# Wider shift, cheaper skip term, one more eight-residue slice and later turned rows in a fused layer-norm, long-convolution and MLP gradient kernel

## The chip, the cores and the metric

The kernel runs on one core of a Trainium2 chip. The metric is device microseconds of a whole execution, as a median over runs. Executions of the kernel before lie between about 1953 and 1974 us here, so a difference of a few microseconds needs many runs or a stage of the trace. All comparisons below are between executions in the fast state, and the one profile that fell in the slow state is marked.

TensorE is PE (its weight load PEld), VectorE is DVE, ScalarE is ACT, GpSimd is POOL, SyncE is SP. Numbers after an L are line numbers; the changed kernel's are two or three lower than those of the kernel before.

## The reference, cut to what matters

```python
# S = 2048 rows, D = 1024 channels, F = 3584; all bf16
def forward(A_q, A_k, A_v, shift_k, ssm_k, ssm_D, w_gate, w_up, w_down):
    xn = layernorm(A_q)
    k_shift = sum(pad(A_k)[t:t + S] * shift_k[:, 3 - t] for t in range(4))   # 4 taps
    kv = k_shift * A_v
    y = irfft(rfft(pad(kv, 2 * S)) * rfft(pad(ssm_k, 2 * S)))[:S]           # long convolution
    y = y + kv * ssm_D                                                     # the skip term
    s = xn * y
    h = (xn @ w_gate) * (xn @ w_up)
    return A_q + s * silu(h @ w_down)
# returned: the output and the gradients of all nine inputs for a given grad_out
```

## The kernel before

The first 550 us hold the gate and up matmuls (`psg<-wslab,U`, 192 tiles of eight matmuls after the start) and, threaded between them, the forward convolution. The channels are worked in eight slices of 128. For each pair of slices VectorE shifts k and multiplies it by v (`kv`). TensorE transforms `kv` and the filter `hx` (`psF`), ScalarE copies the result out of PSUM (`SP`), VectorE finishes the transforms and multiplies the spectra, and TensorE transforms back (`psY`). A slice is transformed with four residues or with eight: eight takes half the TensorE matmuls and more VectorE work. `hN` is the product of gate and up, made on VectorE and transposed by TensorE. The first matmul that reads all of the gated products, `psbm`, ends the stage.

```python
EIGHT = (7,)                                     # slices transformed with eight residues

def load_kv(dp, c):                              # one block of rows of a pair of slices
    k = kst.tile([P, 2, 11, P], BF16, name="k", bufs=2)
    for e in range(2):
        cld_k(k[:, e], c, 2 * dp + e)            # 128 channels, 256 B, at a time
    ...
def shift(dp):
    kv = cx.tile([P, 2, NB, P], BF16, name="kv")
    ...
    for c in range(2):                           # two blocks of rows, 2048 elements an operation
        ...
        tt(acc, k[:, :, 0:8, :], wb(3), MUL)
        for j in (2, 1, 0):
            tt(prod, k[:, :, 3 - j:11 - j, :], wb(j), MUL)
            tt(acc, acc, prod, ADD)
            yield 2.5                            # the amount of work told to the pacing
        tt(kv[:, :, 8 * c:8 * c + 8, :], acc, v..., MUL)
        st(KSHd[...], acc)                       # shifted k, for the backward pass
# cmm(), the transform of one half on TensorE: the skip term is one more matmul,
# a row of constants (one partition) by the row of ssm_D
    if first is not None and k == 0:
        nc.tensor.matmul(ps[:, 0, 0:P], wsc_row[:], first, start=False, stop=True)
# pacing: after every gate/up tile, pump() emits convolution work up to this share of its total
def tick():
    cnt[0] += 1
    pump((20.0 + (F_TOTAL - 20.0) * (cnt[0] + 4) / NT) / F_TOTAL)
# gate/up unit: product on VectorE in its fixed program order; turned five tiles later
def multiply():
    tt(hN[:, 0:n], gut[:, 0, 0:n], gut[:, 1, 0:n], MUL)
    ...
    defer(turn)
# last stage, tap gradients: turned rows loaded one block ahead
    if i < 15:
        kT, dkT = load_turned(i + 1)
```

`tt` keeps VectorE's operations in the order in which the program writes them. So the pacing decides which `hN` product stands behind which convolution operation.

## Time and profile before

| | kernel before |
|---|---|
| time | 1956.21 us median of 3 runs (1956.19 to 1961.06) |
| the profiled execution | 1968.15 us, span 1966.4, fast state |
| TensorE, VectorE, ScalarE, GpSimd busy | 98%, 77%, 33%, 18% |
| `psbm` begins | 549.4 us |
| gradient matmuls `psx<-…,dgut` | 1551.3 to 1947.9 us, with 8.2 us of waits for `dgut` |

The profiled execution is 12 us slower than the median of the timed ones, so a page's span must not be compared with another kernel's median. TensorE's busy time is modelled from its matmul records, and some records are missing: this page counts 10907 of them and 1924.2 us. A second trace of the very same kernel (run `before_again`) counts 11043 and 1931.9 us. So a change of 5 us in that line says nothing by itself. The starts of single tiles and the named waits are firmer.

### The profile page before, as it was taken

What the parts mean: (1) busy time and instruction counts of PE and PEld (TensorE: products, weight loads), DVE (VectorE), ACT (ScalarE), POOL (GpSimd) and SP (SyncE); (2) the same over time, 40 slices, a digit from 0 to 9 for tenths busy, and PEclk for the clock granted to TensorE, in tenths of its full rate; (3) what the DMA queues carried; (4) which work ended last, traced back from release to release, by engine and by line L of the source; (5) the groups of instructions that cost most, each with busy time, mean ns of one, the idle gap of its engine ahead of it and who ended that gap; (6) DMA issues with size and microseconds to landing.
All of it is one profiled execution on the core that took longest, in us unless ns stands there. A gap on an engine that the chain in (4) does not pass through costs nothing.

```text
span 1966.4 us, 27343 instructions
## 1 busy us (share of the span) xinstructions
PE 1924.2 (98%) x10907; PEld 1038.5 (53%) x11043; DVE 1523.9 (77%) x1711; ACT 639.8 (33%) x940; POOL 356.1 (18%) x529
## 2 busy tenths in 40 slices
PE   8999999999999999999999999999999999999989
PEld 4555555555444446666566666664444444444434
DVE  8699999999736555888799899999995404777763
ACT  5664555555432224333222222222212002001122
POOL 3413222121112221000122121021112001111111
PEclk8999999999999999999999999999999999999999
DMA  8967767556799988566778698575796999897993
GB/s 294 303 213 257 240 205 273 194 180 235 266 285 295 287 274 306 187 214 211 253 245 272 236 240 277 189 270 181 222 260 164 149 207 196 162 213 154 190 210 118
DMA packets 454463, 448.62 MB, mean 228 GB/s; under 512 B 282736, under 2 KB 370872, under 8 KB 440384
## 3 DMA queue, kind: packets, MB, share of 16 engines
q1 hardware_dynamic: 393088, 232.86, 47.1%
q0 software_dynamic: 44928, 184.65, 28.2%
q10 hardware_dynamic: 16320, 29.36, 4.1%
q8 instruction: 86, 1.41, 0.3%
q14 instruction: 41, 0.34, 0.1%
HBM read 198.20 MB, written 189.84 MB: 197 GB/s over the span
## 4 chain that ended last, share of the span: by engine, by line
PE 62%; issue 17%; DVE 7%; DMA 5%; POOL 4%; SPq 3%; ACT 2%; another core or an unknown queue 0%; POOLq 0%; ACTq 0%; DVEq 0%
PE psb L1256 19%; PE psb L1332 9%; PE psb L1239 9%; PE psg L617 9%; PE psx L1383 7%; PE psbm L1108 3%; SPq L1327 3%; DVE dkp L1087 2%; PE psF L231 2%; DMA HTd<-hT 1%; DVE dka L209 1%; PE psY L443 1%; DMA xn_t<-XNd 1%; DMA dkT<-DKSHd 1%; DVE W L209 1%
## 5 line engine op out<-in xcount | busy, mean ns | idle before, releaser
L617 PE MATMUL psg<-wslab,U 128*128 128x512 bf16 x1732 | 406.5, 382 | 14.4 <-ACT gut L619 6.2
L1256 PE MATMUL psb<-U,U 128*128 128x512 bf16 x1792 | 397.4, 379 | 0.0
L1383 PE MATMUL psx<-U,dgut 128*128 128x512 bf16 x1507 | 333.1, 380 | 10.5 <-DMA dgut<-DGd 8.2
L1383 PEld LDWEIGHTS <-dgut 128*128 128x128 bf16 x1792 | 175.5, 98 | 222.2 <-DMA dgut<-DGd 9.8
L617 PEld LDWEIGHTS <-U 128*128 128x128 bf16 x1792 | 173.8, 98 | 200.8 <-issue 15.3
L1256 PEld LDWEIGHTS <-U 128*128 128x128 bf16 x1792 | 175.2, 98 | 197.6
L1239 PE MATMUL psb<-wdt,U 128*128 128x256 bf16 x1792 | 205.3, 273 | 1.1 <-ACT bm L1126 1.1
L1239 PEld LDWEIGHTS <-U 128*128 128x128 bf16 x1792 | 175.3, 98 | 32.0 <-issue 1.4
L619 ACT CAST gut<-psg 128x512 bf16<-128x512 f32 x216 | 126.3, 586 | 183.7 <-PE psg L617 172.2
L1332 PE MATMUL psb<-U,U 128*128 128x512 bf16 x813 | 179.6, 379 | 1.0
L1108 PE MATMUL psbm<-U,ht 128*128 128x512 bf16 x768 | 168.9, 379 | 0.8
L1261 ACT CAST wb<-psb 128x512 bf16<-128x512 f32 x112 | 65.6, 586 | 311.1 <-PE psb L1256 295.6
L209 DVE TENSOR_TENSOR W<-W 128x1024 f32<-128x1024 f32 (+1 forms) x150 | 151.3, 1026 | 3.2
L1332 PEld LDWEIGHTS <-U 128*128 128x128 bf16 x896 | 87.4, 98 | 105.4 <-issue 1.0
L1108 PEld LDWEIGHTS <-ht 128*128 128x128 bf16 x784 | 76.6, 98 | 91.8
L1415 ACT ACTIVATE dx_t<-dxn 128x1024 bf16<-128x1024 f32 x15 | 15.9, 1057 | 331.4 <-DVE dxn L209 331.4
L1241 ACT CAST dht<-psb 128x512 bf16<-128x512 f32 x112 | 65.7, 586 | 121.3 <-PE psb L1239 120.2
L209 DVE TENSOR_TENSOR U<-U,dht 128x2048 bf16<-128x2048 bf16 x56 | 68.3, 1221 | 46.2 <-ACT dht L1241 46.1
L1087 DVE SCALAR_TENSOR_TENSOR dkp<-dkT,kT 128x1024 bf16<-128x1024 bf16 (+2 forms) x64 | 78.3, 1224 | 29.1 <-DMA dkT<-DKSHd 27.4
L209 DVE TENSOR_TENSOR dxn<-psx,dxna_t 128x1024 f32<-128x1024 f32 x15 | 18.3, 1222 | 94.7 <-PE psx L1383 80.0
L1362 ACT CAST wbs<-psb 128x512 bf16<-128x512 f32 x52 | 30.5, 586 | 148.2 <-PE psb L1332 139.2
L209 DVE TENSOR_TENSOR W<-SP 128x1024 f32<-128x1024 f32 x64 | 74.2, 1220 | 4.0 <-ACT SP L253 3.1
(243 smaller groups left out, 2383.0 us busy)
## 6 DMA issues: line engine op xcount, KB each, us to landing
U<-GUd SPq DMA_DIRECT2D x28, 1024.0 KB, 8.2
DGd<-U SPq DMA_DIRECT2D x28, 1024.0 KB, 4.8
GUd<-gut ACTq DMA_DIRECT2D x54, 512.0 KB, 5.9
out_dram<-wb SPq DMA_DIRECT2D x112, 128.0 KB, 4.3
U<-Hd SPq DMA_DIRECT2D x14, 1024.0 KB, 5.5
Hd<-hN POOLq DMA_DIRECT2D x54, 256.0 KB, 4.2
HTd<-hT POOLq DMA_DIRECT2D x54, 256.0 KB, 3.3
ht<-HTd SPq DMA_DIRECT2D x7, 1536.0 KB, 9.7
```

The lines of the kernel that those rows point to most:

```text
L209: pinned(V.tensor_tensor(o, a, b, op))
L617: gu_mm[0] = nc.tensor.matmul(ps[:], XNT[q][:, dc, qi * P:(qi + 1) * P], w[:, dc].rearrange("p a f -> p (a f)"), start=(dc == 0), stop=(dc ...
L619: nc.scalar.copy(out=gut[:, :, i], in_=ps[:].rearrange("p (a f) -> p a f", a=2))
L1087: ins = V.scalar_tensor_tensor(prod[:].rearrange("p r d -> p (r d)")[:, lo:H], dkT[:, 0, lo:H], 1.0, kT[:, 0, 13 + m + lo:13 + m + H], op0 ...
L1108: nc.tensor.matmul(ps[:, dh * 512:(dh + 1) * 512], ht(fc)[:, i * P:(i + 1) * P], WD[fc // 4][:, fc % 4, dh * 512:(dh + 1) * 512], start=(f ...
L1239: nc.tensor.matmul(ps[:, x * SLW:(x + 1) * SLW], DBMT[2 * hf + g][:, dc, (b % 4) * P:(b % 4 + 1) * P], wdt[:, dc, :], start=(dc == 0), sto ...
L1241: nc.scalar.copy(out=dht[:, 2 * e:2 * e + 2].rearrange("p b f -> p (b f)"), in_=ps[:])
L1256: nc.tensor.matmul(ps[:], XN[b // 4][:, b % 4, dc * P:(dc + 1) * P], dgus[b // 8][:, :, b % 8], start=(b == 0), stop=(b == NB - 1))
L1261: nc.scalar.copy(out=wb[:, dc % 2].rearrange("p a f -> p (a f)"), in_=ps[:])
L1327: nc.sync.dma_start_transpose(out=t[:, 2 * i:2 * i + 2], in_=DGd[2 * j + i, a, 512 * g:512 * g + 512, :])
L1332: nc.tensor.matmul(ps, h[:, b, f * P:(f + 1) * P], DBM[b // 4][:, b % 4, dh * 512:(dh + 1) * 512], start=(b == 0), stop=(b == NB - 1))
L1383: nc.tensor.matmul(ps[:, dh * 512:(dh + 1) * 512], t[n][:, f, i * P:(i + 1) * P], WGU[n][:, f, dh * 512:(dh + 1) * 512], start=(n == 0 and ...
```

## The change

The change makes the shift work on both slices of a pair and both row blocks at once (256 channels side by side, 4096 elements an operation). The skip term uses the transform's own weights by a row padded to 128 partitions (`Dz`), so no one-row weights are loaded. Slice 0 is also done with eight residues, to take matmuls from TensorE. The turned rows of the tap gradients are loaded later. The pacing constants move with it.

```diff
-    KSHd = dram.tile([8, P, NB, P], BF16, name="KSHd")
-    KSLd = dram.tile([8, S + 8, P], BF16, name="KSLd")
+    KSHd = dram.tile([4, P, NB, 256], BF16, name="KSHd")
+    KSLd = dram.tile([4, S + 8, 256], BF16, name="KSLd")
...
-                nc.tensor.matmul(ps[:, 0, 0:P], wsc_row[:], first, start=False, stop=True)
+                nc.tensor.matmul(ps[:, 0, 0:P], T[:, 0, 0, :], first, start=False, stop=True)
...
-    EIGHT = (7,)
+    EIGHT = (0, 7)
+    SHIFT_W = 8 * 2.3
...
-            for c in range(2):
-                ...                     # eight operations of 2048 elements a block
+            k = S_.pop(("k", dp))
+            wb = lambda j: Wbc[:, j:j + 1, dp * 256:(dp + 1) * 256].unsqueeze(1).to_broadcast([P, 2, 8, 256])
+            acc, prod, v = [U[i][:].rearrange("p (c r d) -> p c r d", c=2, r=8) for i in (6, 7, 4)]
+            with tc.issue_after(last.ins):
+                tt(acc, k[:, :, 0:8, :], wb(3), MUL)
+            yield 2.3
+            for j in (2, 1, 0):
+                tt(prod, k[:, :, 3 - j:11 - j, :], wb(j), MUL)
+                yield 2.3
+                tt(acc, acc, prod, ADD)
+                yield 2.3
+            tt(kv[:].rearrange("p (c r) d -> p c r d", c=2), acc, v, MUL)
+            st(KSHd[dp], U[6][:].rearrange("p (b d) -> p b d", b=NB))
...
+        Dz = cs.tile([P, D], BF16, name="Dz")
+        V.memset(Dz[:], 0.0)
+        cld(Dz[0:1, :], A_ssm_D.rearrange("(o d) -> o d", o=1))
+        nc.scalar.activation(Dz[0:1, :], Dz[0:1, :], ACT.Copy, scale=WSC)
...
-        pump((20.0 + (F_TOTAL - 20.0) * (cnt[0] + 4) / NT) / F_TOTAL)
+        pump((SHIFT_W + (F_TOTAL - SHIFT_W) * (cnt[0] + 8) / (NT + 4)) / F_TOTAL)
...
-        kT, dkT = load_turned(0)
...
+                if j == 2:
+                    kT, dkT = load_turned(i)
...
-            if i < 15:
-                kT, dkT = load_turned(i + 1)
```

More of the change, by code (lines that the diff above doesn't have):

```diff
@@ L74, in build_kernel, with cld_k @@
     cld = st
-    def cld_k(t, c, ds):
-        src = KSLd[ds]
-        cld(t, bass.AP(src.tensor, src.offset + 1024 * c * P, [[8 * P, P], [P, 11], [1, P]]))
+    def cld_k(t, c, dp):
+        src = KSLd[dp]
+        cld(t, bass.AP(src.tensor, src.offset + 1024 * c * 256, [[8 * 256, P], [256, 11], [1, 256]]))
     def cld_v(t, c, d0, w):
@@ L126, in build_kernel @@
     RSTN = const.tile([P, NB], F32, name="RSTN")
-    wsc_row = const.tile([1, P], BF16, name="wsc_row")
-    nc.vector.memset(wsc_row[:], WSC)
     Wbc = const.tile([P, 4, D], BF16, name="Wbc")
@@ L139, in zero_rows @@
         V.memset(zr[:], 0.0)
-        st(KSLd[:, 0:3, :], zr[:, 0:3, :])
+        st(KSLd[:, 0:3, :], zr[0:4].rearrange("p a x -> p (a x)")[:, 0:768].rearrange("p (a x) -> p a x", a=3))
         st(DKSHd[:, S:S + 8, :], zr[:])
@@ L649, in load_kv @@
         def load_kv(dp, c):
-            k = kst.tile([P, 2, 11, P], BF16, name="k", bufs=2)
-            for e in range(2):
-                cld_k(k[:, e], c, 2 * dp + e)
+            if c == 0:
+                S_["k", dp] = kst.tile([P, 2, 11, 256], BF16, name="k")
+            cld_k(S_["k", dp][:, c], c, dp)
             v = U[4][:, 2048 * c:2048 * c + 2048].rearrange("p (a x) -> p a x", a=8)
             cld_v(v, c, dp * 256, 256)
-            S_["kv", dp, c] = (k, v)
         def load_h(ds):
@@ L659, in load_h @@
             cld(U[5][:, 0:2048], A_ssm_k[ds * P:(ds + 1) * P, :])
-            drow = cs.tile([1, P], BF16, name="drow", bufs=2)
-            cld(drow[:], A_ssm_D[ds * P:(ds + 1) * P].rearrange("(o d) -> o d", o=1))
             S_["h", ds] = hrow
-            S_["D", ds] = drow
         def shift(dp):
-            kv = cx.tile([P, 2, NB, P], BF16, name="kv")
+            kv = cx.tile([P, NB, 256], BF16, name="kv")
             S_["kvt", dp] = kv
-            wb = lambda j: Wbc[:, j, dp * 256:(dp + 1) * 256].rearrange("p (e d) -> p e d", e=2).unsqueeze(2).to_broadcast([P, 2, 8, P])
-            for c in range(2):
-                k, v = S_.pop(("kv", dp, c))
-                acc = U[7 - c][:, 0:2048].rearrange("p (e r d) -> p e r d", e=2, r=8)
-                with tc.issue_after(last.ins):
-                    tt(acc, k[:, :, 0:8, :], wb(3), MUL)
-                for j in (2, 1, 0):
-                    prod = U[7][:, 2048:4096].rearrange("p (e r d) -> p e r d", e=2, r=8)
-                    tt(prod, k[:, :, 3 - j:11 - j, :], wb(j), MUL)
-                    tt(acc, acc, prod, ADD)
-                    yield 2.5
-                tt(kv[:, :, 8 * c:8 * c + 8, :], acc, v.rearrange("p r (e d) -> p e r d", e=2), MUL)
-                st(KSHd[2 * dp:2 * dp + 2, :, 8 * c:8 * c + 8, :].rearrange("e u b d -> u e b d"), acc)
-                yield 2.5
+            k = S_.pop(("k", dp))
[11 more added lines that the diff above has]
+            st(KSHd[dp], U[6][:].rearrange("p (b d) -> p b d", b=NB))
+            yield 2.3
         def h_rows(ds):
@@ L699, in kvs @@
         def kvs(ds):
-            return S_["kvt", ds // 2][:, ds % 2]
+            return S_["kvt", ds // 2][:, :, ds % 2 * P:(ds % 2 + 1) * P]
         def tail(ds):
@@ L763, in conv_forward @@
                     load_kv(ds // 2 + 1, c)
-            D0 = S_.pop(("D", ds))[:]
+            D0 = Dz[:, ds * P:(ds + 1) * P]
             sph = []
@@ L796, in conv_forward @@
         kst.release()
-    F_TOTAL = 4 * 20.0 + 6.0 + 8 * (0.5 + FWD4_W + 1.3 + PROD_W + INV_W) + 10.0 - 0.95 * 8 * (4 * 1.75 + 0.95 + 4 * 0.9)
+    F_TOTAL = 4 * SHIFT_W + 6.0 + 8 * (0.5 + FWD4_W + 1.3 + PROD_W + INV_W) + 10.0 - 0.95 * 8 * (4 * 1.75 + 0.95 + 4 * 0.9)
     F_TOTAL += len(EIGHT) * 2 * (FWD8_W - 9.6 + 0.95 * 1.75) - 2.0
@@ L812, in copy_k @@
     def copy_k(dp):
-        for ds in (2 * dp, 2 * dp + 1):
-            ld(KSLd[ds, 3:3 + S, :].rearrange("(p a) d -> p a d", a=16),
-               kin[:, ds * P:(ds + 1) * P].rearrange("(p a) d -> p a d", a=16))
+        ld(KSLd[dp, 3:3 + S, :].rearrange("(p a) d -> p a d", a=16),
+           kin[:, dp * 256:(dp + 1) * 256].rearrange("(p a) d -> p a d", a=16))
     copy_k(0)
@@ L854, in tick @@
         cnt[0] += 1
-        pump((20.0 + (F_TOTAL - 20.0) * (cnt[0] + 4) / NT) / F_TOTAL)
-    pump(20.0 / F_TOTAL)
+        pump((SHIFT_W + (F_TOTAL - SHIFT_W) * (cnt[0] + 8) / (NT + 4)) / F_TOTAL)
+    pump(SHIFT_W / F_TOTAL)
     for sl in range(2, NSL - 2):
@@ L972, in load_side @@
                 cld_v(v[:, 8 * c:8 * c + 8, :], c, ds * P, P)
-            cld(ksh[:], KSHd[ds])
+            cld(ksh[:], KSHd[ds // 2][:, :, ds % 2 * P:(ds % 2 + 1) * P])
             side_in[n] = (v, ksh)
```

## The prediction

> **What bounds the kernel now.** I read the page first (busy shares, then the chain that ended last), then busy time by stretch, then the two engines' instruction timelines where their stretches are full.
>
> The page's first line of part 1:
> ```profile
> PE 1924.2 (98%) x10907; PEld 1038.5 (53%) x11043; DVE 1523.9 (77%) x1711; ACT 639.8 (33%) x940; POOL 356.1 (18%) x529
> ```
> TensorE idles only 42 us of 1966.4 in the whole span. So the kernel is TensorE-bound on average. An average over stages hides a second limit, so next the busy times by stretch (columns: length, then busy us and instruction count of PE, PEld, DVE, ACT, POOL; clock; DMA share; GB/s):
> ```profile
> 92.00:200.00 108.00, 103.86 (x665) 59.81 (x676) 102.52 (x92) 60.48 (x82) 26.46 (x42) 1.00 0.75 244
> 200.00:300.00 100.00, 99.36 (x618) 56.77 (x629) 98.78 (x88) 55.82 (x78) 22.73 (x35) 1.00 0.67 228
> 300.00:400.00 100.00, 99.14 (x630) 57.64 (x641) 95.67 (x85) 57.16 (x80) 22.73 (x35) 1.00 0.62 219
> 400.00:545.00 145.00, 140.87 (x838) 77.19 (x852) 126.46 (x124) 75.90 (x111) 26.91 (x41) 1.00 0.68 232
> 545.00:765.00 220.00, 216.71 (x1096) 107.04 (x1114) 116.67 (x181) 61.91 (x66) 45.53 (x71) 1.00 0.95 298
> ```
> From 92 to 400 us, the stage in which the gate/up matmuls run beside the forward convolution, TensorE and VectorE are both full: 98.78 of 100 us of VectorE between 200 and 300. After 545 VectorE is half idle. Three of the four parts of the change act in that doubly full stage. The timelines show how the two are tied there (start, length, engine, line, operation; the wait in brackets):
> ```profile
> 193.02 0.61 PE L637 MATMUL tr<-ident,hN 128*128 128x128 bf16 x8
> 195.04 1.91 PE L231 MATMUL psF<-kv,TF 128*128 128x256 bf16 x16 [1.42 <-DVE kv L209]
> ...
> 193.76 1.23 DVE L209 TENSOR_TENSOR kv<-U,U 128x2048 bf16<-128x2048 bf16 x1
> ...
> 302.26 1.22 DVE L209 TENSOR_TENSOR kv<-U,U 128x2048 bf16<-128x2048 bf16 x1
> 303.93 1.91 PE L231 MATMUL psF<-kv,TF 128*128 128x256 bf16 x16
> ```
> TensorE starts on `kv` (the shifted k times v) at 195.04, when VectorE has just finished it at 194.99; the next pair is finished at 303.48 and used at 303.93. Both queues keep a fixed order, so there is next to no slack: what lengthens VectorE's work ahead of `kv` moves TensorE.
>
> **What the Trainium skill says.** "VectorE: DVE Perf Modes", Side-by-side: where the cycles go for N=2048 bf16, gives 1224 ns for a two-source bf16 operation of 2048 elements, with about 150 cycles of it fixed; the trace agrees (1218 to 1225 ns for 2048, 2284 ns for 4096). So joining two operations saves one fixed part, not half. "TensorEngine Tiling (Array Packing)", Key Properties, says that changing the tiling mode drains TensorE. The trace fits: each load of the one-row skip weights sits idle 0.21 us first. "DMA: Bandwidth & Descriptors", Specifications, puts line rate at 512 B and above; the page counts 282736 of 454463 packets under 512 B, but no wait of TensorE in this stage names the k copies.
>
> **The change, part by part.**
>
> 1. Shift. 16 operations of 2048 elements a pair of slices become 8 of 4096. One half before took 184.60 to 194.91 with one `hN` product of 0.60 in it: 9.7 us, so 19.4 us a pair; eight at 2284 ns are 18.3 us. It saves about 1.1 us of VectorE a pair, 4.4 in all, 3.3 of it after the first pair (which lies before 85 us, where VectorE waits for TensorE anyway).
>
> 2. Skip term on the transform's own weights.
> ```profile
> L236 PE MATMUL psF<-drow,wsc_row x15: 224/224/226, 99.6 to 473.1; 1*128 1x128 bf16 x15
> its engine sat idle before it (us, times) until:
>   issue: 3.1, 15
> ```
> Around one of them: two transform matmuls start at 138.72, the skip term at 139.04, the next at 139.19. Two transform matmuls cost 0.22 (16 take 1.75 from start to start), so 0.47 minus 0.22 leaves 0.25 us a term; a full-height 128-column one costs about 0.06 (8 transposes take 0.44). That saves about 0.2 us on 14 terms (one of 15 goes): 3.0 us of TensorE. The row is now loaded into a zeroed 128-row tile and scaled on ScalarE. In the built program that scaling stands in ScalarE's fixed order between two gate/up evictions and waits for the load, which waits for the clearing on VectorE. I put the clearing at about 78 us and the landing 4.1 us (the old row's median) after the issue; TensorE may wait 1 us there.
>
> 3. First slice with eight residues. TensorE loses 32 transform matmuls of 256 columns (16 on `kv`, 16 on `hx`) at 0.109 us: 3.5 us. VectorE gains: in the old kernel the last slice is already done so, and its first transform runs from 470.44 to 486.78 with one `hN` product inside, 15.7 us; the four-residue transform of slice 0 runs from 98.07 to 107.34, 9.3 us. Two transforms: +12.9 us.
>
> 4. Later turned rows. In the built program the sync queue holds the turned loads at the same places between the same `dgut` loads, and each still waits for the last tap product of the unit before. The added store waits are for stores half a millisecond old. VectorE's order after the forward stage is unchanged. I give it 0. The one large wait of the last stage therefore stays:
> ```profile
> 1882.84 0.61 PE L1383 MATMUL psx<-U,dgut 128*128 128x512 bf16 x1 [5.68 <-DMA dgut<-DGd]
> ```
> The k copies and loads get 512 B rows (off the path), while the backward reads of the stored shift get 256 B rows, 2048 a load, hidden behind prefetch.
>
> Sum for the forward stage: TensorE -6.5 us; VectorE +12.9 - 3.3 = +9.6 us after its restart at 98.07. Which of them counts is the whole question. The program's order answers: before the third slice's `kv` the changed TensorE queue has about 6.6 us more work than the old (102 against 95, from 0.216, 0.109 and 0.056 us a matmul), because the pacing puts more gate/up work there; VectorE has 12.9 - 1.1 + 0.6 (one more `hN`) = 12.4 more. TensorE, which waited 1.42 there, is now 5.8 us more ahead and waits about 7. For the pairs after it TensorE has some 6 and 4.5 us less work, VectorE only 1.1 less, so it falls short by some 4 us and 3 us again. VectorE's lag of 9 to 10 us is what remains at 415 us. It takes back part: before, it stood 2.33, 1.18 and 1.80 us waiting for gate/up evictions (315.60, 357.54, 469.83), and such waits shrink when it is the late one: -3 to -4. The stage should end 6 us later, give or take 4, with the skip row's wait in it. After 549 us TensorE is full to 1866 us, and there the delay is kept: 1956.2 + 6 = 1962. I shade it to 1961 because the pacing constants look tuned for this order.
>
> **Rivals.**
> A. TensorE alone bounds, VectorE's lag being absorbed. For it: 98% busy, and VectorE stands 5.97 and 10.15 us at the stage's end. That would give 1956.2 - 6.5 = 1950. Against: those waits lie behind the last transforms, and the `kv` hand-overs come earlier.
> B. The later turned rows free the transposing queue and the 8.2 us that TensorE waits for `dgut` between 1866 and 1898 go, alone or on top of A: 1948 or 1942. Against: queue order and waits are the same.
> C. VectorE's lag is paid in full (no waits taken back) and the skip row holds an eviction longer than thought: 1956.2 + 10 + 2 = 1968.
> D. 256 B reads in the backward stage delay its loads: VectorE has 537 of 597 us there, but TensorE waits for nothing of it; under 2 us.
>
> **Range and chances.** Most weight lies on +3 to +10, a quarter on A or a mixture, little on B and C: 1951 to 1969. A move of 2% is 39 us, six times any term, and the old runs spread by 5 us: faster 0.005, same 0.985, slower 0.01.
>
> **What would show it.** Right: in the changed profile TensorE's busy time falls by about 6 us and its waits from 92 to 550 us grow by more than 10, named after VectorE (`kv`, `hN`, `HX`) or ScalarE evictions behind it; the third slice's `kv` comes near 208; VectorE is at 98% or more of 100 to 400; the skip term's idle (3.1 us) is gone; the psbm matmuls begin near 555 instead of 549.4; from there to the end the two traces have equal length within 3 us. Wrong: psbm begins before 549, so VectorE had slack that I don't see; or the `dgut` wait near 1882 vanishes, so part 4 was not inert.

## The result, and the profile after

The changed kernel took 1966.23 us (median of 4 runs, 1963.6 to 1969.7). The kernel before took 1956.2 us in the same rounds (4 runs, 1955.88 to 1961.06). The ratio of the fast runs is 1.0047, with a 95% interval of 1.0024 to 1.0069: within 2%, but slower. (A ratio here is the mean time of one kernel's fast runs over that of the other's of the same rounds, so it is not quite the ratio of the medians.) The profiled execution took 1965.88 us, in the fast state.

The page's first line, with busy time, share and instructions of each engine:

```profile
PE 1919.2 (98%) x10875; PEld 1037.1 (53%) x11010; DVE 1532.7 (78%) x1703; ACT 639.6 (33%) x941; POOL 350.1 (18%) x510
```

VectorE has 8.8 us more than before (1523.9). Then the busy times by stretch (length; busy us and count of PE, PEld, DVE, ACT, POOL; clock; DMA share; GB/s):

```profile
92.00:200.00 108.00, 102.39 (x630) 57.03 (x640) 102.39 (x102) 58.14 (x81) 19.97 (x31) 0.98 0.65 216
200.00:300.00 100.00, 97.05 (x611) 56.65 (x620) 99.14 (x83) 55.50 (x77) 23.50 (x36) 0.98 0.73 244
300.00:400.00 100.00, 96.65 (x615) 56.63 (x626) 96.98 (x80) 56.03 (x78) 22.25 (x34) 1.00 0.65 225
```

VectorE is now the fuller of the two from 200 to 400 us, and TensorE has gaps. Two things are to be seen: TensorE's busy time falls below VectorE's, and the granted clock is 0.98 in two stretches where it was 1.00. The hand-over of the second pair, VectorE first and TensorE second (start, length, engine, line, operation, the wait in brackets):

```profile
206.34 2.29 DVE L207 TENSOR_TENSOR kv<-U,U 128x4096 bf16<-128x4096 bf16 x1
...
208.68 2.43 PE L229 MATMUL psF<-kv,TF 128*128 128x256 bf16 x16 [2.17 <-DVE kv L207]
...
315.54 1.91 PE L229 MATMUL psF<-kv,TF 128*128 128x256 bf16 x16 [1.92 <-DVE kv L207]
```

`kv` comes at 208.6, where it came at 195.0. TensorE waits 2.17 us for it, and 1.92 us for the next one, which before cost nothing. The waits of TensorE by cause, before (92 to 550 us) and after (92 to 556 us), with total, times and longest; smaller ones are left out:

```profile
PE psg L617 <- ACT gut L619: 2.8, 2, 2.2
PE psF L231 <- ACT SP L253: 1.8, 1, 1.8
PE psF L231 <- DVE kv L209: 1.4, 1, 1.4
PE tr L637 <- ACT hT L638: 1.1, 1, 1.1
PE tr L637 <- DVE hN L209: 0.4, 1, 0.4
...
```

```profile
PE tr L635 <- DVE hN L207: 5.6, 2, 3.3
PE psF L229 <- DVE kv L207: 4.8, 3, 2.2
...
PE psg L615 <- ACT gut L617: 0.6, 1, 0.6
...
```

The waits named after VectorE grew from 1.8 to 10.4 us; those for ScalarE's `gut` fell from 2.8 to 0.6. The largest is one that no hand-over of `kv` shows. VectorE had eight-residue work of slice 0 queued ahead of an `hN` product that TensorE needed:

```profile
114.79 4.63 DVE L207 TENSOR_TENSOR W<-SP 128x1024 f32<-128x1024 f32 x4
119.34 0.69 DVE L207 TENSOR_TENSOR hN<-gut 128x1024 bf16<-128x1024 bf16 x1
...
120.08 0.62 PE L635 MATMUL tr<-ident,hN 128*128 128x128 bf16 x8 [3.29 <-DVE hN L207]
120.74 3.18 PE L615 MATMUL psg<-wslab,U 128*128 128x512 bf16 x8
```

The eight matmuls after the wait take 3.18 us, where eight take 1.89 elsewhere. The stretches of 3 us after it say why; the third number from the end is the granted clock:

```profile
120.00:123.00 3.00, 2.88 (x15) 1.42 (x16) 2.97 (x5) 1.99 (x3) 1.17 (x2) 0.70 0.23 87
123.00:126.00 3.00, 3.00 (x18) 1.73 (x17) 2.96 (x6) 0.58 (x1) 0.10 (x1) 0.74 0.25 87
126.00:129.00 3.00, 2.95 (x15) 1.37 (x14) 3.00 (x6) 1.17 (x2) 0.56 (x1) 1.00 0.24 89
```

After standing still for 3.29 us TensorE runs at 0.70 and 0.74 for two stretches. That is (1 − 0.70) × 3 + (1 − 0.74) × 3 = 1.7 us more, on top of the wait. The Trainium skill has this effect: "TensorE: Matmul & The Clock Gate", What's actually happening, says that the array's clock is halved after an idle window of about 3.4 us and restored after a busy one. The size fits this trace: by an estimate from the page's figure, half speed for 3.4 us costs 1.7 us. What starts it does not quite fit; see the last section.

The ends of the stages, from the list of one tile's instructions (median duration, first and last start):

```profile
L1105 PE MATMUL psbm<-U,U x110: 379/379/379, 555.6 to 579.6; 128*128 128x512 bf16 x110
...
L1380 PE MATMUL psx<-U,dgut x1507: 376/379/380, 1558.8 to 1945.4; 128*128 128x512 bf16 x189
```

`psbm` begins at 555.6 instead of 549.4. The gradient matmuls take 386.6 us instead of 396.6, because in this execution they do not wait for `dgut`. That is why the two profiled spans (1966.4 and 1964.1) go the other way than the timed medians.

### An account of the forward stage

For every trace I split the time from the first gate/up matmul to `psbm` in three. Waits are what the profile's list of TensorE's waits sums to in that stretch. Clock is (1 − granted clock) times length, summed over stretches of 20 us. The rest is what TensorE's work takes at full clock. The rest scatters by up to 3 us among traces with the same TensorE work (515.2 to 518.1 in the first four rows).

| run | length | waits | clock | rest |
|---|---|---|---|---|
| kernel before | 539.1 | 17.5 | 6.4 | 515.2 |
| before_again (the same kernel) | 537.8 | 16.3 | 3.4 | 518.1 |
| only_turned | 540.1 | 16.7 | 8.2 | 515.2 |
| only_shift | 536.2 | 18.4 | 0.0 | 517.8 |
| only_skip | 540.2 | 22.8 | 3.4 | 514.0 |
| eight7 | 544.4 | 22.5 | 8.8 | 513.1 |
| eight7_pace | 538.6 | 20.2 | 5.0 | 513.4 |
| changed kernel | 545.3 | 27.2 | 8.8 | 509.3 |
| after_pace | 540.9 | 24.3 | 5.0 | 511.6 |
| less_dve | 538.7 | 21.9 | 5.4 | 511.4 |
| less_dve2 | 535.9 | 18.5 | 5.4 | 512.0 |
| three8 | 555.4 | 35.9 | 12.2 | 507.3 |
| pool_gate | 574.7 | 46.8 | 17.6 | 510.3 |

From before to changed: rest −5.9, waits +9.7, clock +2.4, together +6.2 us. Of the waits' 9.7, 1.6 are waits for the first weights (`wslab`), which vary from 0 to 3.2 us among the traces.

After `psbm`, the fast traces with under 2 us of waits for `dgut` need 1407 to 1411 us to the end of the span, the changed kernel's 1408.5 included. The kernel before needed 1417.0 in its profiled execution and 1422.1 in before_again, less_dve2 1417.6.

### The profile page after: what moved, and what is told of

It is laid out like the page before. It is cut to its first block, busy times and chain, and to the rows that moved or that the text cites. A ratio compares the mean times of both kernels' runs of the same rounds, so it can differ in the third digit from the quotient of the medians.

```text
span 1964.1 us, 27240 instructions
## 1 busy us (share of the span) xinstructions
PE 1919.2 (98%) x10875; PEld 1037.1 (53%) x11010; DVE 1532.7 (78%) x1703; ACT 639.6 (33%) x941; POOL 350.1 (18%) x510
## 4 chain that ended last, share of the span: by engine, by line
PE 72%; issue 12%; DVE 8%; DMA 3%; POOL 3%; ACT 1%; another core or an unknown queue 0%; SPq 0%; POOLq 0%; ACTq 0%; DVEq 0%
PE psx L1380 20%; PE psb L1253 19%; PE psb L1329 9%; PE psb L1236 9%; PE psbm L1105 6%; PE psg L615 5%; DVE W L207 2%; DVE U L207 1%; DVE HX L207 1%; PE psF L229 1%; DVE KX L207 1%; PE psY L1034 1%; DMA XNd<-U 1%; PE psY L430 1%; DMA U<-in_A_v_dram 1%
## 5 line engine op out<-in xcount | busy, mean ns | idle before, releaser
L207 DVE TENSOR_TENSOR W<-W 128x1024 f32<-128x1024 f32 (+1 forms) x156 | 156.5, 1020 | 3.4
## 6 DMA issues: line engine op xcount, KB each, us to landing
GUd<-gut ACTq DMA_DIRECT2D x54, 512.0 KB, 5.5
```

The lines of the kernel that those rows point to most:

```text
L207: pinned(V.tensor_tensor(o, a, b, op))
```

## The experiments

Twelve kernels ran in three groups, each group on one chip with its own runs of the kernel before (medians 1959.41, 1958.74 and 1958.13 us; 46, 67 and 43 runs). The theory is that VectorE's extra work for slice 0 lengthens the forward stage. The rivals are the new layout, the skip row, the pacing, the turned rows, and TensorE alone.

"First `kv` to `psbm`" runs from the end of VectorE's first whole `kv` to the start of `psbm`: 464.7 us in the kernel before (465.2 in before_again), 473.7 in the changed kernel. The changed kernel's first `kv` ends 2.8 us sooner after the first gate/up matmul (71.6 against 74.4 us), so this measure shows a loss of 9.0 us where the whole stage shows 6.2.

### before_again: what two executions of one kernel differ by

No edit.

> The old kernel once more, for the spread and for the wait for dgut. Its first profile held 8.2 us of waits for dgut after 1866 us and a time of 1968.15, while its timed runs were at 1956. Theory: the wait belongs to that one execution; this profile has less than 2 us of it and a span near 1955. Rival: the wait is a fixed part of the kernel, and returns with 6 to 9 us. The ratio to the old kernel should be 1.000 within 0.002.

Measured: 1958.9 us (14 runs), ratio 1.0001 (0.9986 to 1.0017). Its profiled execution took 1970.45 us and waited for `dgut` again, six times:

```profile
PE psx L1383 <- DMA dgut<-DGd: 6.9, 6, 2.7
```

My expectation of under 2 us was wrong. Eight other fast traces, some with the old loads (only_shift, only_skip) and some with the new, have no such wait. So it comes and goes from execution to execution, and one pair of profiles can't show that a change removed it. Still, waits of more than 2 us in total were seen only with the old loads, in 2 of 4 fast traces, and in none of 9 with the new; that the later loads make the wait rarer isn't excluded.

### only_eight: part 3 alone

```diff
-    EIGHT = (7,)
+    EIGHT = (0, 7)
```

> The old kernel with eight residues in the first slice as the only change. Theory: VectorE +12.9, TensorE -3.5, and no shift to take 3.3 back: psbm starts 8 to 11 us later than the old 549.4, the time is 1964 to 1968, as bad as the whole change or worse. Rival (TensorE bounds): 3.5 us faster, 1952 to 1953.

Measured: 1964.4 us (17 runs), ratio 1.0025 (1.0015 to 1.0034). The theory's 1964 is just met, but over this group's base of 1959.41: the loss is 4.9 us by the ratio, half of the whole change's 9.2, and not "as bad or worse". The rival's 1952 is out: with 3.5 us less for TensorE to do the kernel is slower. (`EIGHT` also enters `F_TOTAL`, the total of the pacing, so the pacing shifts a little with it.) Its profiled run fell in the slow state (1990.55 us), so I take nothing from its trace.

### only_shift: part 1 alone

The change's `KSHd`, `KSLd`, `load_kv` and `shift` with `EIGHT = (7,)`, the old pacing offset, skip row and turned rows.

> The kernel before with part 1 of the change alone (two slices side by side, 256 channels a row; old residues, old pacing offset, old skip row, old turned rows). Theory (the extra eight-residue slice on VectorE is the whole loss, and the new layout is harmless or a little good): VectorE busy 2 to 5 us less than before (1523.9), TensorE busy unchanged within 1.5 us of 1924, first kv to the gate matmuls (psbm) 463 to 465 us against 464.7 and 465.2 for the kernel before, time within 3 us of it. Rival (the layout itself costs: one wait for both row blocks, U6/U7/U4 freed later, 256-byte reads in the last stage): first kv to psbm 468 or more, or psbm to the end of the last gradient matmuls 4 us or more longer than before.

Measured: 1958.62 us (22 runs), ratio 1.0010 (0.9991 to 1.0029). VectorE is busy 1519.6 us, 4.3 less. First `kv` to `psbm` took 464.5 us. The layout is harmless and no gain: the saved VectorE time is not where the path is, since here TensorE waits for `kv` only 0.2 us. There is a small cost before the first `kv`: TensorE's wait for `gut` near 74 us is 3.3 to 4.0 us in all nine fast traces with the new shift and 2.0 to 2.5 in the four with the old.

### only_skip: part 2 alone

```diff
-                nc.tensor.matmul(ps[:, 0, 0:P], wsc_row[:], first, start=False, stop=True)
+                nc.tensor.matmul(ps[:, 0, 0:P], T[:, 0, 0, :], first, start=False, stop=True)
```

with the row `Dz` made as in the change.

> The kernel before with part 2 alone (skip term on row T[:,0,0,:], one padded row tile Dz made once by ScalarE). Theory: TensorE busy about 3 us less (15 one-row weight loads with 0.2 us of idle each go, on the slices that use four residues), and the idle put down to issue before these matmuls disappears; but the stage is held by VectorE as well, so first kv to psbm shortens by 0 to 2 us and the time stays within 3 us of before. Rival (TensorE alone bounds): first kv to psbm 3 us shorter. Second rival (waiting for Dz on ScalarE): a TensorE wait of 1 us or more between 76 and 106 us named after Dz.

Measured: 1962.56 us (22 runs), ratio 1.0014 (0.9997 to 1.0031); first `kv` to `psbm` 464.3 us. The new skip matmuls stand in the profile of the changed kernel with nothing listed under the idle time before them:

```profile
L234 PE MATMUL psF<-Dz,TF x14: 219/219/219, 100.0 to 480.0; 128*128 128x128 bf16 x14
its engine sat idle before it (us, times) until:
```

The 3.1 us of idle are gone, here and in only_skip. The rest of only_skip's stage is 514.0 us, 2.6 below the mean of the four traces with the old skip row and the old slices (516.6). Yet the time is not shorter: waits took its place (22.8 against 17.5 us). No wait is named after `Dz`, but the largest comes from it. ScalarE's fixed order has the scaling of `Dz` before a gate/up eviction:

```profile
82.04 1.05 ACT L718 ACTIVATE Dz<-Dz 1x1024 bf16<-1x1024 bf16 x1 [4.59 <-DVE U L207]
83.01 1.03 ACT L617 CAST gut<-psg 128x512 bf16<-128x512 f32 x2
...
83.61 5.18 PE L615 MATMUL psg<-wslab,U 128*128 128x512 bf16 x16 [3.80 <-ACT gut L617]
```

The row's load was issued at 75.2 us and took 6.7 to land, to 81.9: ScalarE stood for it (the view names a VectorE operation instead), the eviction came late, and TensorE waited 3.80 us and then ran at a clock of 0.80 for 8 us. So the second rival's wait was there, under another name. In the eight other fast traces with `Dz` the load took 3.1 to 4.4 us, ScalarE stood before the scaling for at most 1.1 us, and TensorE has no such wait. How often the load is late can't be said from one trace.

### only_turned: part 4 alone

The change's last two hunks on the kernel before.

> The kernel before with part 4 alone (turned rows of the tap gradients loaded after the first of three row products, not one block ahead). Theory: nothing before the last stage changes; the last stage (first to last gradient matmul of psx) keeps its length of some 386 us plus whatever the transposes of dgut wait, which come and go from execution to execution; time within 3 us of before. Rival (the later loads are what took the dgut wait away in the changed kernel): no dgut wait above 1 us in the profile and timed median 5 us or more below before.

Measured: 1958.35 us (14 runs), ratio 1.0001 (0.9989 to 1.0013). The gradient matmuls took 386.6 us without a `dgut` wait, and the median is where it was. The rival needed a median 5 us lower. Part 4 has no effect on the time beyond the interval, some 2.5 us either way.

### eight7 and eight7_pace: without part 3, with the new and the old pacing

eight7 is the changed kernel with

```diff
-    EIGHT = (0, 7)
+    EIGHT = (7,)
```

and eight7_pace has in addition the old offsets (the new `SHIFT_W`, 18.4 for 20, stays):

```diff
-        pump((SHIFT_W + (F_TOTAL - SHIFT_W) * (cnt[0] + 8) / (NT + 4)) / F_TOTAL)
+        pump((SHIFT_W + (F_TOTAL - SHIFT_W) * (cnt[0] + 4) / NT) / F_TOTAL)
```

> The changed kernel with the first slice back at four residues (only the last slice has eight); shift, skip term, turned rows and the changed pacing stay. Theory (VectorE's extra 12.9 us in the forward stage is what the change costs): VectorE falls by 13 us, TensorE rises by 3.5; the psbm matmuls start near 549 to 551 instead of 555.6, the time falls by 5 to 8 us against the changed kernel, to 1956 to 1960 (the changed pacing is too early for it: TensorE should wait some 5 us at the third slice's kv). Rival 1 (another part costs it, such as the skip row on ScalarE or the new layout): the time stays at 1964 to 1970. Rival 2 (the extra time lies in the last stage): psbm comes earlier but the time does not fall with it.

> As the run before, and the pacing put back to the old offsets (tick plus 4 over 192). Theory: now both engines have less work than in the old kernel (TensorE -3.0 us, VectorE -3.3 us) and no hand-over is late by more than 2 us, so psbm starts near 546 and the time is 3 to 4 us under the old kernel's, 1952 to 1953, and 13 us under the changed kernel's. Rival (the pacing does not matter): the same time as the run before within 1 us.

Measured: eight7 1970.46 us (6 runs), ratio 1.0056 (1.0035 to 1.0077); eight7_pace 1959.47 us (22 runs), ratio 1.0005 (0.9987 to 1.0022). Both missed. I had expected that taking slice 0 back would repair the changed kernel, and with the new pacing it does not. In eight7 the convolution runs ahead of the tiles, and TensorE reaches the rows of slice 1's filter before they have landed; later it stands before a `gut` eviction:

```profile
101.69 0.33 PE L685 MATMUL tr<-ident,U 128*128 128x128 bf16 x1 [4.91 <-DMA U<-in_A_ssm_k_dram]
...
236.45 6.77 PE L615 MATMUL psg<-wslab,U 128*128 128x512 bf16 x24 [3.04 <-ACT gut L617]
```

Both are followed by low clock (24 gate/up matmuls take 5.34 us elsewhere, 6.77 here). So the pacing is a cost of its own, which the prediction did not list as a part. VectorE is as light here (1520.3 us) as in less_dve below (1521.5), which loses nothing: where VectorE is relieved matters too. With the old pacing the loss is gone, but there is no gain of 3 us either: the rest is 3.2 us below the mean of 516.6, which is the skip term's part, and the waits are 2.7 us above those of the kernel before.

### after_pace: the changed kernel with the old pacing

The same hunk on the changed kernel.

> The changed kernel with the old pacing offset (count + 4 of NT) in place of the new one (count + 8 of NT + 4): nothing else. Theory (VectorE's load decides, pacing only says which wait it shows as): first kv to psbm 471 to 475 against 473.7, time within 3 us of the changed kernel. Rival (the earlier pacing costs here what it cost in eight7 against eight7_pace, 8 us): first kv to psbm 468 or less.

Measured: 1961.63 us (22 runs), ratio 1.0019 (1.0007 to 1.0032); first `kv` to `psbm` 468.6 us. This lies between the two: my theory's 471 is missed, and the rival's 468 is not quite reached. What stays of the loss is 3.9 of 9.0 us from first `kv` to `psbm`, 1.8 of 6.2 in the whole stage, and 0.19 of 0.47% by the ratios. So half or more of the loss hangs on the new pacing. The wait of 3.29 us for `hN` at 120.08 isn't there, and the 2.32 us for `hN` at 520 has shrunk to 1.51; the waits for `kv` stay (6.1 us in all). In VectorE's fixed order an `hN` product now stands before the block of slice 0 that it stood behind in the changed kernel:

```profile
111.46 0.69 DVE L207 TENSOR_TENSOR hN<-gut 128x1024 bf16<-128x1024 bf16 x1
...
113.39 4.63 DVE L207 TENSOR_TENSOR W<-SP 128x1024 f32<-128x1024 f32 x4
```

So the new pacing puts slice 0's work ahead of `hN`. Set side by side, all with the new shift, skip row and loads (ratio with its interval; length of the stage):

| | old offsets | new offsets |
|---|---|---|
| slice 0 with four residues | eight7_pace: 1.0005 (0.9987 to 1.0022); 538.6 us | eight7: 1.0056 (1.0035 to 1.0077); 544.4 us |
| slice 0 with eight | after_pace: 1.0019 (1.0007 to 1.0032); 540.9 us | changed kernel: 1.0047 (1.0024 to 1.0069); 545.3 us |

The new offsets cost 4.4 to 5.8 us of the stage. Slice 0's eight residues cost 2.3 us with the old offsets and 0.9 with the new, both within the scatter of single traces; by the ratios, with the new offsets they cost nothing that shows. The ratios come from different rounds, so the sizes are rough.

### less_dve and less_dve2: the changed kernel with less for VectorE to do

Wrong results on purpose; TensorE's work stays.

```diff
-                tt(prod, k[:, :, 3 - j:11 - j, :], wb(j), MUL)
+                n = 1 if j == 0 and dp > 0 else 8          # less_dve2: j < 2
+                tt(prod[:, :, 0:n], k[:, :, 3 - j:3 - j + n, :], wb(j)[:, :, 0:n], MUL)
...
-                tt(acc, acc, prod, ADD)
+                tt(acc[:, :, 0:n], acc[:, :, 0:n], prod[:, :, 0:n], ADD)
```

> The changed kernel with one of the seven VectorE steps of the pair's shift cut to an eighth for pairs 1 to 3 (wrong result on purpose: one tap missing on most rows), so that VectorE has some 10 us less to do in the forward stage while TensorE's order and work stay. Theory (VectorE's extra 9 us is what lengthened the stage): VectorE busy about 1522, TensorE busy as after (1919), first kv to psbm falls from 473.7 back to 463 to 467. Rival (the changed pacing offset, or the first slice's place in the TensorE order, lengthens it whatever VectorE does): first kv to psbm stays at 470 or more.

> As less_dve, but two of the three taps are cut to an eighth for pairs 1 to 3 (wrong result on purpose), so VectorE has about 20 us less in the forward stage than the changed kernel. Theory (what the change saves on TensorE is real and only VectorE hides it): first kv to psbm falls below the kernel before's 464.7 to 465.2, to 457 to 461, which is TensorE's 6.5 us. Rival (less_dve's 466.1 is already TensorE's floor, so the TensorE saving never was there, or goes in its waits for gut and in its lower clock before 120 us): first kv to psbm stays at 464 or more.

Measured: less_dve 1958.57 us (22 runs), ratio 1.0003 (0.9990 to 1.0016), VectorE 1521.5 us, first `kv` to `psbm` 466.1 us. The theory holds: with the pacing and the order of slice 0 as changed, 11 us less on VectorE, in the later pairs' shifts, take the loss away. It does not follow that VectorE's extra work alone made the loss: eight7, without that work, keeps it. The hand-over that TensorE waited 2.17 us for has shrunk to this:

```profile
203.93 1.91 PE L229 MATMUL psF<-kv,TF 128*128 128x256 bf16 x16 [0.38 <-DVE kv L207]
```

less_dve2: 1956.18 us (22 runs), ratio 0.9996 (0.9981 to 1.0011), VectorE 1510.8 us, first `kv` to `psbm` 463.4 us. Neither expectation is met in full. TensorE's saving is real (the rest is 512.0, 4.6 us below the mean of 516.6), but even with VectorE 22 us lighter than in the changed kernel the waits (18.5 us) are no fewer than before. The 3.28 us for `hN` at 118.25 and 3.80 us for `gut` at 73.77 stand before the first of the lightened shifts, so these two kernels pay them too.

### three8: a third eight-residue slice

```diff
-    EIGHT = (0, 7)
+    EIGHT = (0, 4, 7)
```

> The changed kernel with a third eight-residue slice, slice 4, where VectorE is as full as TensorE. Theory (each such slice costs the stage what it adds to VectorE, and gives back nothing of what it takes from TensorE): VectorE busy about 1545 (+12.9), TensorE about 3 less, first kv to psbm 482 to 488 against 473.7, time 8 to 14 us above the changed kernel. Rival (the first slice is special: its extra VectorE work falls where the queue starts and cannot be hidden, a middle slice's can): first kv to psbm within 3 us of 473.7.

Measured: 1977.3 us (6 runs), ratio 1.0094 (1.0073 to 1.0115), VectorE 1545.4 us, first `kv` to `psbm` 483.2 us. The theory's numbers for VectorE, the stage and the time hold (TensorE's rest, 507.3, is 2.0 below the changed kernel's); the rival, that slice 0 is special, is out. TensorE's two largest waits in the stage, 92 to 565 us:

```profile
PE tr L635 <- DVE hN L207: 11.6, 3, 5.7
PE psF L229 <- DVE kv L207: 6.1, 3, 2.2
```

### pool_gate: a correct kernel that relieves VectorE

The experiments suggest that relieving VectorE could make the change pay. GpSimd is 18% busy, so I moved half of the `hN` products to it.

```diff
-            tt(hN[:, 0:n], gut[:, 0, 0:n], gut[:, 1, 0:n], MUL)
+            if n == 4 and b0 % 8 == 4:
+                nc.gpsimd.tensor_tensor(hN[:, 0:n], gut[:, 0, 0:n], gut[:, 1, 0:n], MUL)
+            else:
+                tt(hN[:, 0:n], gut[:, 0, 0:n], gut[:, 1, 0:n], MUL)
```

> The changed kernel, correct, with 27 of the products of gate and up halves (hN) done by GpSimd, which is 18% busy, in place of VectorE: 27 x 0.68 us = 18 us less on VectorE in the forward stage. Theory (VectorE binds): if GpSimd is not in VectorE's way, first kv to psbm 458 to 464 and a time up to 6 us below the kernel before. Rival: GpSimd's products take several us each, hold back its own DMA issues (HTd, Hd, k, v) and slow VectorE's instructions beside them; then the VectorE rows for k and Wbc lengthen from 2.29 us and psbm comes no earlier than in the changed kernel.

Measured: 1994.02 us (5 runs), ratio 1.0186 (1.0160 to 1.0211), `psbm` at 583.6 us. The rival holds, as far as it was looked at (GpSimd's own DMA issues were not). Some groups of instructions of this run, 92 to 550 us (busy us, mean ns):

```profile
L626 POOL TENSOR_TENSOR hN<-gut 128x1024 bf16<-128x1024 bf16 x22 | 60.7, 2758 | 21.4 <-ACT gut L617 21.1
...
L207 DVE TENSOR_TENSOR U<-k,Wbc 128x4096 bf16<-128x4096 bf16 x12 | 29.1, 2437 | 0.2
L207 DVE TENSOR_TENSOR m<-KX,HX 128x2048 bf16<-128x2048 bf16 x16 | 27.1, 1730 | 0.0
```

A product takes 2758 ns on GpSimd against 684 ns on VectorE. Worse, the group of VectorE's spectrum products shown last takes 1730 ns where the changed kernel has 1218 (three other groups of 2048 elements take 1445 to 1471 against 1220 to 1225): VectorE is busy 1561.2 us in all, 28.5 more than in the changed kernel, although 28 products have left it. The Trainium skill names the mechanism in "SBUF — State Buffer", Who interferes with whom: a VectorE instruction with two inputs in SBUF contends with a GpSimd instruction that reads SBUF. The trace agrees with a lengthening of 42% of that group; whether each long one met a GpSimd product was not looked at.

No run beat the kernel before by more than its interval. Among the correct ones only_turned, only_shift, only_skip and eight7_pace can't be told from it, so there is no better version to offer.

## Why the prediction was right or wrong, point by point

**What bounds the kernel.** Right in that the forward stage is where the change acts and that VectorE is as much a limit as TensorE there: only_eight, less_dve and three8 show it in three ways. VectorE's load is not the whole of it: eight7 has none of the extra work and is no faster than the changed kernel.

**Part 1.** Right in size (4.3 us of VectorE in only_shift, 4.4 predicted) and in being no gain by itself.

**Part 2.** The idle of 3.1 us went, as predicted, and no time came of it. The 1 us wait for the row on ScalarE did not occur in the changed kernel, where the row landed before ScalarE came to it; in only_skip it occurred with 3.80 us. The mechanism was right, and its size depends on when the load lands.

**Part 3.** Right in its sizes. VectorE rose by 8.8 us in all; the parts give 12.9 − 4.4 = 8.5. Slice 4 in three8 added 12.7 us, against 12.9 for slice 0. For TensorE the rest fell by 5.9 us (6.5 predicted; 5.5 if four traces of each kind are averaged: (515.2 + 518.1 + 515.2 + 517.8) / 4 less (509.3 + 511.6 + 511.4 + 512.0) / 4). That these sizes make the loss was only in part right; see the pacing.

**Part 4.** Right that it is worth 0, shown by only_turned. The sentence that the one large wait of the last stage therefore stays was wrong: it was absent from the changed kernel's profile, and my own sign for a wrong prediction came on. The sign was a bad one, since a kernel can have the wait in some executions and not in others (5.68 us in the old loads' trace, none in only_shift's). With it fell the sign that the two traces are equally long from `psbm` on within 3 us: 1417.0 and 1408.5.

**The sum for the stage.** `kv` near 208: 208.6. `psbm` near 555: 555.6. But the way there was not as told. I had TensorE wait about 7 us at the third slice's `kv`, then 4 and 3; it waited 2.17, then 1.92 and 0.7. By then it had lost 3.29 us at `hN` and some 1.7 to the clock, which with the 2.17 make 7.2: about the foretold lag, paid in part at a place that the prediction did not name. I had its waits from 92 to 550 us grow by more than 10; from 92 us to `psbm` they grew by 6.1 (7.8 to 13.9); the other 3.6 of the account's 9.7 lie before 92 us. What fills the gap is the term that I left out: a longer wait often costs clock too. From the first `kv` to `psbm` the clock term was 0.0 before and 5.2 us after, with waits of 3.29, 2.17 and 2.32 us followed by some 1.7 us each. (Before the first `kv` the clock term fell by 2.9, from 6.3 to 3.4, so over the whole stage it grew by 2.4 only.) That the sum came out right was luck: one missing term offset waits that I had put too high.

**The pacing.** The prediction used the new pacing only as a reason why more gate/up work stands before the third slice's `kv`, and then took a microsecond off because the constants looked tuned. This is the step of the prediction that failed: the pacing was taken for granted, and it is half or more of the loss (eight7 against eight7_pace, changed against after_pace). The shading was wrong in sign. With the old constants the changed kernel is nearer to the kernel before (after_pace), and with the new ones it runs into an `hN` product queued behind slice 0's transform.

**The total.** 1961 was predicted and 1966.23 measured, inside the range. Against the same rounds' 1956.2 the ratio makes +9.2 us (its interval 4.7 to 13.5), where +5 was forecast. One microsecond of the gap is the shading. The base may be another part: 1956.2 rests on 4 runs, and the later groups of 43 to 67 runs have 1958.1 to 1959.4. The stage's +6.2 us on those gives 1964 to 1966. That isn't shown, and a share of slower stages in the timed runs may be in it too; only one execution of the changed kernel was traced, so this stays open. One sum of the prediction is wrong, without effect: 39 us is three times its largest term (12.9), not six times any.

**The rivals.** A (TensorE alone bounds) is out: only_eight. B (the `dgut` wait goes with part 4) is out: only_turned. C (full lag and a costly skip row) has a total, 1968, that is nearer to the measured time than mine, but not its reasons: the skip row's wait did not occur in the changed kernel, and the stage grew by 6.2 us, not 12. D (256 B reads in the backward pass) is out: from `psbm` to the end only_shift needs 1408.2 us, as kernels with the old reads do (only_turned 1407.0, only_skip 1411.4).

## What to carry to other kernels

When two engines are full in the same stage, moving work from one to the other can cost more than it saves, whatever the average shares say; test it by making the receiving engine lighter, even with a wrong result, and by taking the work back. Then cross the parts of a change: here the pacing mattered more than the part that was held to be the cost. An operation order fixed in the program makes pacing a part of the change: look at which small product stands behind which long block. Judge a change of a few microseconds by the start of a stage's first tile and by many timed runs, not by the spans of two profiles.

## What the Trainium skill lacked or had wrong

- "TensorE: Matmul & The Clock Gate" puts the clock drop at an idle window of about 3.4 us. Here waits from 2.0 us on already bring it. In the 13 fast traces (waits of 0.9 us and more from 55 to 600 and from 1850 to 1960 us; a mean clock under 0.9 in the 8 us after each) the drop followed 11 of 16 waits of 2 to 3 us (2.17 us at 208.68 among them), 21 of 23 longer ones, and 3 of 57 under 2 us. The usual cost of one is 1.7 us, so a wait of 2 us costs nearly double when the drop comes. For the short, frequent idles that it blames in one other kernel the page gives no length.
- "SBUF — State Buffer" says who contends; the ratios that the pages give for GpSimd against VectorE are for single cases, none for a mix like this: 2758 ns for a GpSimd product of 128x1024 bf16 against 684 ns on VectorE, and 1445 to 1730 against 1218 to 1225 ns for four groups of VectorE operations of 2048 elements in the same stage.
- No page says how far matmul records and busy time of one kernel differ between two traces: 10907 and 11043 records, 1924.2 and 1931.9 us busy here.
- "TensorEngine Tiling (Array Packing)" says that a change of tiling mode drains TensorE, without a duration: if that is what stood here, it was 0.21 us of idle before each one-row skip term, and it was gone when the rows were full height.
